# Splitting the MLP of a decode step into four column groups that overlap across engines

## The chip, the cores and the metric

The kernel runs on one core of a Trainium2 chip. A core has engines that each run their own instruction stream in order: TensorE (matrix multiplies and transposes, written PE in the profile, with its weight loads as PEld), VectorE (DVE), ScalarE (ACT), GpSimd (POOL) and SyncE (SP). They wait for each other on semaphores. DMA queues move data between main memory (HBM) and the on-chip SBUF; TensorE writes its results to PSUM. The metric is the device time of one execution in microseconds (us). Five executions of the kernel before have a median of 883.75 us (882.21 to 885.1).

## The reference

One decode step (one token each for 8 sequences) through two identical layers. x has 8 rows of 640 values. Each layer is an attention with a key and value cache and then an MLP, both with a layer norm ahead and a residual add behind:

```python
W = min(4096, max(256, Sk // 4))          # 1024 of 4096 cached positions
q = (x @ wq)                              # 32 heads of 128
scores = einsum("bhqd,bhkd->bhqk", q, k) * (Dh ** -0.5)
o = einsum("bhqk,bhkd->bhqd", softmax(scores), v)
return o @ wo

def _B_ref(x, w1, b1, w2, b2):
    y = _layernorm(x, axis=-1)
    h = _gelu(einsum("bsd,df->bsf", y, w1) + b1)     # tanh form, F = 1728
    return einsum("bsf,fd->bsd", h, w2) + b2
...
x = x + _A_ref(_layernorm(x, axis=-1), A_k_cache, A_v_cache, A_wq, A_wo)
x = x + _B_ref(_layernorm(x, axis=-1), B_w1, B_b1, B_w2, B_b2)
x = x + _A_ref(_layernorm(x, axis=-1), A_k_cache, A_v_cache, A_wq, A_wo)
x = x + _B_ref(_layernorm(x, axis=-1), B_w1, B_b1, B_w2, B_b2)
```

Both layers use the same weights and the same caches. The caches' last 1024 positions amount to some 134 MB, which are read once per attention.

## The kernel before

The program emits attention, MLP, attention, MLP (`emit_A`, `emit_B`, lines 733 to 736). Each `emit_` function adds blocks to the engines' streams, and on each engine the order of the blocks is the order of execution. Every dependency is a semaphore wait written by hand: `S_DVM`, `S_ACM` and `S_PEM` count finished steps of VectorE, ScalarE and TensorE in the parts outside the attention's loop.

**Attention** (lines 285 to 648). It walks 32 chunks, each being 8 heads of one sequence, with 2 MB of K and 2 MB of V. There are three K buffers and two V buffers. K transfers are issued by SyncE (L592), V transfers by ScalarE (L509). In each chunk VectorE computes the scores of six heads by a multiply and reduce (L346), and TensorE those of two, by transposing K (L413), a copy on ScalarE (L531) and a product (L423). ScalarE takes the exponentials, TensorE multiplies with V (L447). The layer starts with the queries (L366, evacuated by L499, spread over the partitions by L380 and L519) and ends with the output projection L631 and the residual add L640. SyncE starts the K transfers of layer 2 as soon as the projection L631 of layer 1 is done, so before the MLP. The first V transfer of layer 2 comes behind the second L499 in ScalarE's stream.

**Layer norm** (`emit_ln_yt`, L221 to L283) is shared by both kinds of layer. Two sums on ScalarE (L227, L229), five tiny steps on VectorE, a logarithm and an exponential with their table loads (L248, L250), the normalised rows YBF (L262), five transposes (L271) and their copy to YTS (L278). Then VectorE builds SELB, eight selector matrices (L281), which the attention's broadcast L380 uses. The function returns VectorE's count after SELB, and TensorE waits for that count before it uses YTS.

**MLP** (`emit_B`, L650 to L731). In the order in which it runs:
- L662: y @ w1 into HP, 8 rows of 1728 fp32 values in PSUM. Five chunks of the inner size 640 accumulate, in column pieces of at most 512; twenty matmuls.
- L671 to L677 on VectorE, over all 1728 columns: add B1 (result UB in bf16), square, multiply by 0.044715 and add 1, multiply by UB.
- L683 on ScalarE: tanh. L690 and L692 on VectorE: half of tanh plus a half, times UB, into HBF.
- L701: fourteen transposes bring HBF's 128-column pieces to partitions (HT_PS). L708 and L709 copy them to HTS.
- L720: HTS @ w2 into O2_PS, 8 rows of 640; fourteen matmuls of 512 columns and then fourteen of 128.
- L728 adds the residual, L730 adds B2.

Each step waits for the whole of the one before. UB, SELB and the layer norm's scratch lie in the same memory (UF). HP lies in PSUM tensor P4, HT_PS in TPS; MPS is used only by the attention.

Of the kernel before, what the change touches and what calls it, by code (L numbers as in the profile page):

```python
# [8 lines left out]
BF16 = mybir.dt.bfloat16  # L9
I32 = mybir.dt.int32  # L10
ALU = mybir.AluOpType
ACTF = mybir.ActivationFunctionType
# [16 lines left out]
def bass_interleave_layers__sliding_block_cached__mixer_channel_mlp__decode_kernel(  # L29
# [13 lines left out]
    B, Sq, D = A_x.shape  # L43
# [11 lines left out]
    DC = D // 128  # L55
# [21 lines left out]
    with es:  # L77
# [76 lines left out]
        HT_PS = TPS[:, 64:64 + FC * 8]  # L154
        TPOSB = TPS[:, 256:384]
        TPOS = [TPOSA, TPOSB]
        DEN_PS = [ACC[0:1, 512:512 + H * J], ACC[0:1, 768:768 + H * J]]
        WO_PS = ACC[0:8, 0:D]
        O2_PS = ACC[0:8, 0:D]
# [58 lines left out]
            S_DVM.inc(v.tensor_single_scalar(IDENT128[:, :], IOTA128[:, :], 0, ALU.is_equal))  # L218
        DVM_IDENT = S_DVM.count

        def emit_ln_yt(xin, x_ready_waits):  # L221
            @block.scalar
            def _(sc):
                for s, cval in x_ready_waits:
                    sc.wait_ge(s.handle, cval)
                sc.wait_ge(S_ACM.handle, S_ACM.count)
                S_ACM.inc(sc.activation(JUNK[:, :], xin[0:B, :], ACTF.Identity, accum_out=STAT[:, 0:1]))  # L227
                sc.wait_ge(S_ACM.handle, S_ACM.count)
                S_ACM.inc(sc.activation(JUNK[:, :], xin[0:B, :], ACTF.Square, accum_out=STAT[:, 1:2]))  # L229
            acm_stat = S_ACM.count  # L230

            @block.vector
            def _(v):
                v.wait_ge(S_ACM.handle, acm_stat)
                S_DVM.inc(v.tensor_scalar(STAT[:, 2:3], STAT[:, 0:1], 1.0 / D, None, ALU.mult))
                S_DVM.inc(v.tensor_scalar(STAT[:, 3:4], STAT[:, 1:2], 1.0 / D, None, ALU.mult))
                v.wait_ge(S_DVM.handle, S_DVM.count)
                S_DVM.inc(v.tensor_tensor(STAT[:, 4:5], STAT[:, 2:3], STAT[:, 2:3], ALU.mult))
                v.wait_ge(S_DVM.handle, S_DVM.count)
                S_DVM.inc(v.tensor_tensor(STAT[:, 5:6], STAT[:, 3:4], STAT[:, 4:5], ALU.subtract))  # L240
                v.wait_ge(S_DVM.handle, S_DVM.count)
                S_DVM.inc(v.tensor_scalar(STAT[:, 6:7], STAT[:, 5:6], 1e-5, None, ALU.add))
            dvm_var = S_DVM.count

            @block.scalar
            def _(sc):
                sc.wait_ge(S_DVM.handle, dvm_var)
                S_ACM.inc(sc.activation(STAT[:, 6:7], STAT[:, 6:7], ACTF.Ln))  # L248
                sc.wait_ge(S_ACM.handle, S_ACM.count)
                S_ACM.inc(sc.activation(STAT[:, 6:7], STAT[:, 6:7], ACTF.Exp, scale=-0.5))  # L250
            acm_sqrt = S_ACM.count

            @block.vector
            def _(v):
                v.wait_ge(S_ACM.handle, acm_sqrt)
                S_DVM.inc(v.scalar_tensor_tensor(STAT[:, 7:8], STAT[:, 2:3], -1.0, STAT[:, 6:7], ALU.mult, ALU.mult))
            dvm_nmr = S_DVM.count

            @block.scalar
            def _(sc):  # L260
                sc.wait_ge(S_DVM.handle, dvm_nmr)
                S_ACM.inc(sc.activation(YBF[0:B, :], xin[0:B, :], ACTF.Identity, bias=STAT[:, 7:8], scale=STAT[:, 6:7]))  # L262
            acm_y = S_ACM.count

            @block.tensor
            def _(t):
                t.wait_ge(S_ACM.handle, acm_y)
                t.wait_ge(S_DVM.handle, DVM_IDENT)
                ins = None
                for c in range(DC):  # L270
                    ins = t.transpose(YT_PS[:, c * 8:c * 8 + 8], YBF[0:B, c * 128:(c + 1) * 128], IDENT128[0:B, 0:B])  # L271
                S_PEM.inc(ins)
            pem_yt = S_PEM.count

            @block.vector
            def _(v):
                v.wait_ge(S_PEM.handle, pem_yt)
                S_DVM.inc(v.tensor_copy(YTS[:, :, 0:B], YT_PS[:, 0:DC * 8].rearrange("p (c b) -> p c b", c=DC)))  # L278
                ins = None
                for b in range(B):  # L280
                    ins = v.tensor_copy(SELB[0:8, b, :], IDENT128[0:8, b:b + 1].to_broadcast([8, 128]))  # L281
                S_DVM.inc(ins)
            return S_DVM.count  # L283

        def emit_A(xin, xout, x_ready):
# [362 lines left out]
            return dvm_x  # L648

        def emit_B(xin, xout, x_ready):  # L650
            dvm_yts = emit_ln_yt(xin, x_ready)

            @block.tensor
            def _(t):
                t.wait_ge(S_DVM.handle, dvm_yts)
                t.wait_ge(WA_W1[0].handle, WA_W1[1])
                ins = None
                n0 = 0
                while n0 < F:
                    n1 = min(n0 + 512, F)  # L660
                    for c in range(DC):
                        ins = t.matmul(HP[0:8, n0:n1], YTS[:, c, :], W1[:, c, n0:n1], start=(c == 0), stop=(c == DC - 1))  # L662
                    n0 = n1
                S_PEM.inc(ins)
            pem_hp = S_PEM.count

            @block.vector
            def _(v):
                v.wait_ge(S_PEM.handle, pem_hp)
                v.wait_ge(WA_B[0].handle, WA_B[1])  # L670
                S_DVM.inc(v.tensor_tensor(UB[0:B, :], HP[0:B, 0:F], B1[0:B, :], ALU.add))  # L671
                v.wait_ge(S_DVM.handle, S_DVM.count)
                S_DVM.inc(v.tensor_tensor(VBF[0:B, :], UB[0:B, :], UB[0:B, :], ALU.mult))
                v.wait_ge(S_DVM.handle, S_DVM.count)
                S_DVM.inc(v.tensor_scalar(VBF[0:B, :], VBF[0:B, :], 0.044715, 1.0, ALU.mult, ALU.add))
                v.wait_ge(S_DVM.handle, S_DVM.count)
                S_DVM.inc(v.tensor_tensor(VBF[0:B, :], VBF[0:B, :], UB[0:B, :], ALU.mult))  # L677
            dvm_v = S_DVM.count

            @block.scalar  # L680
            def _(sc):
                sc.wait_ge(S_DVM.handle, dvm_v)
                S_ACM.inc(sc.activation(VBF[0:B, :], VBF[0:B, :], ACTF.Tanh, scale=GELU_C))  # L683
            acm_s = S_ACM.count

            @block.vector
            def _(v):
                v.wait_ge(S_ACM.handle, acm_s)
                with nc.allow_low_precision("gelu bf16 intermediates"):
                    S_DVM.inc(v.tensor_scalar(VBF[0:B, :], VBF[0:B, :], 0.5, 0.5, ALU.mult, ALU.add))  # L690
                v.wait_ge(S_DVM.handle, S_DVM.count)
                S_DVM.inc(v.tensor_tensor(HBF[0:B, :], VBF[0:B, :], UB[0:B, :], ALU.mult))  # L692
            dvm_h = S_DVM.count

            @block.tensor
            def _(t):
                t.wait_ge(S_DVM.handle, dvm_h)
                ins = None
                for k in range(FC):
                    cols = 128 if k < FC - 1 else F_LAST  # L700
                    ins = t.transpose(HT_PS[0:cols, k * 8:k * 8 + 8], HBF[0:B, k * 128:k * 128 + cols], IDENT128[0:B, 0:B])  # L701
                S_PEM.inc(ins)
            pem_ht = S_PEM.count

            @block.vector
            def _(v):
                v.wait_ge(S_PEM.handle, pem_ht)
                S_DVM.inc(v.tensor_copy(HTS[:, 0:FC - 1, 0:B], HT_PS[:, 0:(FC - 1) * 8].rearrange("p (k b) -> p k b", k=FC - 1)))  # L708
                S_DVM.inc(v.tensor_copy(HTS[0:F_LAST, FC - 1, 0:B], HT_PS[0:F_LAST, (FC - 1) * 8:FC * 8]))  # L709
            dvm_hts = S_DVM.count  # L710

            @block.tensor
            def _(t):
                t.wait_ge(S_DVM.handle, dvm_hts)
                t.wait_ge(WA_W2[0].handle, WA_W2[1])
                ins = None
                for (n0, n1) in [(0, 512), (512, D)]:
                    for k in range(FC):
                        rows = 128 if k < FC - 1 else F_LAST
                        ins = t.matmul(O2_PS[0:8, n0:n1], HTS[0:rows, k, :], W2[0:rows, k, n0:n1],  # L720
                                       start=(k == 0), stop=(k == FC - 1))
                S_PEM.inc(ins)
            pem_o2 = S_PEM.count

            @block.vector
            def _(v):
                v.wait_ge(S_PEM.handle, pem_o2)
                S_DVM.inc(v.tensor_tensor(xout[0:B, :], xin[0:B, :], O2_PS[0:B, 0:D], ALU.add))  # L728
                v.wait_ge(S_DVM.handle, S_DVM.count)
                S_DVM.inc(v.tensor_tensor(xout[0:B, :], xout[0:B, :], B2[0:B, :], ALU.add))  # L730
            return S_DVM.count  # L731

        dvm_x1 = emit_A(XT[0], XT[1], [(S_GD, 16)])
# [43 lines left out]
```

The softmax here doesn't subtract the row's maximum and nothing guards it: scores larger than these inputs give would overflow.

## Time and profile before

| | |
|---|---|
| median of 5 executions | 883.75 us (882.21 to 885.1) |
| span of the profiled execution | 879.6 us |
| busy, share of the span | TensorE 532.2 us (60%), VectorE 726.3 (83%), ScalarE 353.4 (40%) |
| data moved by DMA | 290.16 MB, mean 330 GB/s |
| first MLP: W1's first matmul to the last add's end | 424.59 to 447.32 us |
| second MLP: the same | 854.39 to 877.33 us |
| layer norm of the first MLP, up to W1's start | 417.06 to 424.59 us |

How to read it: the page divides the span into 40 slices of 22 us. A digit is an engine's busy share of a slice in tenths; PEclk is the granted TensorE clock in tenths of full speed; GB/s is what the DMA engines moved. The chain of work that ended last follows each instruction back to what released it. In a list of instructions or of the chain, the first number is the start, the second the duration in us, and "x20" a group of twenty. A matmul's row lasts longer than its share of the stream since matmuls are pipelined. In a table of stretches come, after the stretch's length, the busy time of each engine with its count of instructions (TensorE, weight loads, VectorE, ScalarE, GpSimd, or one engine alone), the granted clock, the DMA share and GB/s.

### The profile page before, as it was taken

How to read it: one execution, taken by the hardware profiler on the slowest of the kernel's cores; microseconds unless marked ns; L12 is line 12 of the kernel's file. 1: busy time of each engine (PE TensorE's matmuls, PEld its weight loads, DVE VectorE, ACT ScalarE, POOL GpSimd, SP SyncE). 2: the span in 40 equal slices, each digit the busy share in tenths (PEclk: the TensorE clock that was granted, in tenths of full speed). 3: DMA queues.
4: the chain of work that ended last, by engine and by line, in shares of the span. 5: the costliest groups of instructions: out<-in, count | busy, mean ns of one | idle time of the engine just before them, and what ended most of it. 6: DMA issues, size and time to landing. Idle time of an engine off the chain costs nothing.

```text
span 879.6 us, 23392 instructions
## 1 busy us (share of the span) xinstructions
PE 532.2 (60%) x6964; PEld 304.8 (35%) x6964; DVE 726.3 (83%) x6264; ACT 353.4 (40%) x1337; POOL 4.0 (0%) x11
## 2 busy tenths in 40 slices
PE   0866656565656566656358776656565656566364
PEld 0433333333333333333114443333333333333221
DVE  1499999999999999992319999999999999999513
ACT  3454444444444444430235544444444444444120
POOL 1000000000000000000000000000000000000000
PEclk9955555555555555557666555555555555555577
DMA  9999999999999999993706999999999999999700
GB/s 370 381 386 386 385 376 381 364 372 362 373 369 372 363 378 376 373 351 106 280 18 238 356 386 386 386 383 376 364 363 369 372 363 373 362 365 376 253 1 0
DMA packets 143071, 290.16 MB, mean 330 GB/s; under 512 B 2256, under 2 KB 10464, under 8 KB 142304
## 3 DMA queue, kind: packets, MB, share of 16 engines
q1 hardware_dynamic: 74864, 144.72, 44.8%
q10 hardware_dynamic: 67248, 139.50, 43.5%
q0 software_dynamic: 832, 4.44, 1.3%
q8 instruction: 55, 0.90, 0.4%
q14 instruction: 72, 0.59, 0.2%
HBM read 288.64 MB, written 0.01 MB: 328 GB/s over the span
## 4 chain that ended last, share of the span: by engine, by line
DVE 79%; DMA 7%; PE 6%; issue 4%; ACT 3%; DVEq 1%; ACTq 0%
DVE SCRD L346 72%; DVE MLPSCR L346 4%; DMA WQ<-in_A_wq_dram 3%; PE ACC L631 2%; DMA KVALL<-in_A_v_cache_dram 2%; PE P L662 1%; DMA KVALL<-in_A_k_cache_dram 1%; PE ACC L720 1%; DMA KVALL<-in_A_wo_dram 1%; DVE DSUM L317 1%; DVE RDEN L319 1%; DVEq L345 0%; DVE UF L671 0%; ACT L250 0%; ACT L248 0%
## 5 line engine op out<-in xcount | busy, mean ns | idle before, releaser
L346 DVE CUSTOM_DVE_ANT_0 SCRD<-KVALL,QBCB 128x128 bf16<-128x128 bf16 x3072 | 683.2, 285 | 57.9 <-DMA KVALL<-in_A_k_cache_dram 20.3
L346 DVE DVE_READ_ACCUMULATOR2_ANT MLPSCR<- 128x1 f32 x3072 | 246.2, 80 | 0.2
L531 ACT ACTIVATE KTS<-P 128x128 bf16<-128x128 bf16 x512 | 141.8, 277 | 161.8 <-PE P L413 57.5
L519 ACT ACTIVATE QBCB<-P 128x512 bf16<-128x512 f32 x128 | 69.4, 594 | 218.7 <-DVE MLPSCR L346 212.9
L380 PE MATMUL P<-QROWS,UF 8*128 8x512 bf16 x128 | 62.4, 577 | 137.8 <-ACT QBCB L519 136.4
L531 ACT ACTIVATE KTS<-TPS 128x128 bf16<-128x128 bf16 x512 | 139.7, 273 | 4.4
L413 PE MATMUL TPS<-IDENT,KVALL 128*128 128x128 bf16 x512 | 139.9, 273 | 0.0
L413 PE MATMUL P<-IDENT,KVALL 128*128 128x128 bf16 x512 | 138.8, 271 | 0.5 <-DMA KVALL<-in_A_k_cache_dram 0.5
L447 PE MATMUL MPS<-MLPSCR,KVALL 128*128 128x1 bf16 x4096 | 119.0, 165 | 25.4 <-DMA KVALL<-in_A_v_cache_dram 24.5
L423 PE MATMUL P<-QCOL,KTS 128*128 128x1 bf16 x512 | 91.5, 187 | 57.4 <-ACT KTS L531 56.0
L447 PEld LDWEIGHTS MPS<-MLPSCR,KVALL 128*128 128x128 bf16 x4096 | 114.2, 104 | 30.2 <-issue 19.7
L423 PE MATMUL ACC<-QCOL,KTS 128*128 128x1 bf16 x512 | 91.6, 187 | 51.8 <-ACT KTS L531 50.5
L423 PEld LDWEIGHTS P<-QCOL,KTS 128*128 128x128 bf16 x512 | 53.7, 105 | 119.5 <-ACT KTS L531 110.7
L423 PEld LDWEIGHTS ACC<-QCOL,KTS 128*128 128x128 bf16 x512 | 53.7, 105 | 114.9 <-ACT KTS L531 106.2
L380 PEld LDWEIGHTS P<-QROWS,UF 8*128 8x128 bf16 x128 | 12.2, 99 | 165.3 <-issue 142.6
L413 PEld LDWEIGHTS P<-IDENT,KVALL 128*128 128x128 bf16 x512 | 59.6, 116 | 27.5 <-issue 26.9
L413 PEld LDWEIGHTS TPS<-IDENT,KVALL 128*128 128x128 bf16 x512 | 59.9, 117 | 0.0
L366 PE MATMUL P<-WQ,YTS 128*8 128x512 bf16 x80 | 21.8, 437 | 11.1 <-DMA WQ<-in_A_wq_dram 9.7
L227 ACT ACTIVATE UF<-XT 8x640 f32<-8x640 f32 x4 | 2.9, 735 | 53.1 <-DVE XT L640 39.5
L631 PE MATMUL ACC<-KVALL,OTS 128*8 128x128 bf16 (+1 forms) x128 | 20.7, 327 | 3.3 <-DMA KVALL<-in_A_wo_dram 2.1
L271 PE MATMUL TPS<-IDENT,YBF 8*128 8x8 bf16 x20 | 1.2, 167 | 34.0 <-ACT YBF L262 34.0
L550 ACT ACTIVATE MLPSCR<-MLPSCR 128x48 bf16<-128x48 f32 x64 | 15.6, 244 | 15.2 <-DVE MLPSCR L346 15.2
(65 smaller groups left out, 172.2 us busy)
## 6 DMA issues: line engine op xcount, KB each, us to landing
KVALL<-in_A_k_cache_dram SPq DMA_DIRECT2D x64, 2048.0 KB, 17.6
KVALL<-in_A_v_cache_dram ACTq DMA_DIRECT2D x64, 2048.0 KB, 18.4
KVALL<-in_A_wo_dram SPq DMA_DIRECT2D x4, 1920.0 KB, 12.7
WQ<-in_A_wq_dram ACTq DMA_DIRECT2D x1, 5120.0 KB, 22.1
KVALL<-in_A_wo_dram SPq DMA_DIRECT2D x2, 1280.0 KB, 16.8
W<-in_B_w_dram POOLq DMA_DIRECT2D x1, 2160.0 KB, 16.9
W<-in_B_w_dram POOLq DMA_DIRECT2D x1, 2080.0 KB, 23.9
W<-in_B_w_dram POOLq DMA_DIRECT2D x1, 80.0 KB, 23.6
```

The source lines that it names most:

```text
L317: S_DVM.inc(v.tensor_reduce(out=DSUM[:, :], in_=den[0:1, 0:H * J].rearrange("p (h j) -> p h j", j=J), axis=AXX, op=ALU.add))
L319: v.reciprocal(out=RDEN[:, (pb - bt0) * H:(pb - bt0 + 1) * H], in_=DSUM[:, :])
L346: ins = v.tensor_tensor_reduce(out=SCRD[:, slot, :], in0=k_buf[:, hh, j, :], in1=QBCB[gc % 2][:, hh, :], scale=SCALE, scalar=0.0, op0=ALU. ...
L366: ins = t.matmul(QRPS[gq % 2][0:8, 0:QG * Dh], YTS[:, c, :], WQ[:, c, qg * QG * Dh:(qg + 1) * QG * Dh], start=(c == 0), stop=(c == DC - 1))
L380: S_QBM.inc(t.matmul(QPS[qb % 2][:, :], SELB[0:8, b, :], QROWS[0:8, (g * HC + hf * QG) * Dh:(g * HC + (hf + 1) * QG) * Dh], start=True, st ...
L413: S_TP.inc(t.transpose(TPOS[n % 2][:, 0:128], k_buf[:, hh, j, :], IDENT128[:, :]))
L423: S_PQ.inc(t.matmul(SCPS[gc % 2][:, col:col + 1], KTS[n % 2][:, :], QCOL[:, h, b:b + 1], start=True, stop=True))
L447: ins = t.matmul(OTP[:, col:col + 1], v_buf[:, hh, j, :], PB[bt % 2][:, h * J + j:h * J + j + 1], start=(j == 0), stop=(j == J - 1))
L519: S_QEB.inc(sc.activation(QBCB[gc % 2][:, hf * QG:(hf + 1) * QG, :], QPS[qb % 2][:, :].rearrange("p (h d) -> p h d", h=QG), ACTF.Copy))
L531: S_KTE.inc(sc.activation(KTS[n % 2][:, :], TPOS[n % 2][:, 0:128], ACTF.Copy))
L550: S_EXP.inc(sc.activation(PB[bt % 2][:, g * HC * J:(g * HC + hdv) * J], SB[bt % 2][:, g * HC * J:(g * HC + hdv) * J], ACTF.Exp))
L631: ins = t.matmul(WO_PS[0:8, n0:n1], OTS[:, h * 8:h * 8 + 8], WO(h)[:, n0:n1], start=(h == 0), stop=(h == H - 1))
```

## The change

The MLP is split into four groups of columns (512, 512, 512, 192). The aim is that the gelu of one group runs on VectorE and ScalarE while TensorE works on another, and that TensorE's second product starts before the whole gelu is done. Its parts:

- `emit_ln_yt` gets a switch, and the MLP no longer builds SELB.
- W1's matmuls keep their order, but count a semaphore after each group.
- VectorE runs the steps in the order of `ORDER_V`: F is the front (add B1, square, polynomial, product), T the tail after tanh, C the copy of the transposes. TensorE runs X (transposes of a group) and D (its products with W2, both column pieces) in the order of `ORDER_P`. ScalarE takes the tanh by group.
- The transposes alternate between TPS and MPS, so that one group's can be written while another's are copied.
- Four matmuls into MPS ahead of the first X, and seven into P4 ahead of the first D, compute nothing that is used; they are there to keep TensorE active.
- B2 is added to the residual right after the layer norm instead of at the end, so that one add is left there.

```diff
+        HT_PSS = [HT_PS, MPS.bitcast(BF16)[:, 0:FC * 8]]
...
-        def emit_ln_yt(xin, x_ready_waits):
+        def emit_ln_yt(xin, x_ready_waits, build_sel=True):
...
-                ins = None
-                for b in range(B):
-                    ins = v.tensor_copy(SELB[0:8, b, :], IDENT128[0:8, b:b + 1].to_broadcast([8, 128]))
-                S_DVM.inc(ins)
+                if build_sel:
+                    ins = None
+                    for b in range(B):
+                        ins = v.tensor_copy(SELB[0:8, b, :], IDENT128[0:8, b:b + 1].to_broadcast([8, 128]))
+                    S_DVM.inc(ins)
...
+            dvm_yts = emit_ln_yt(xin, x_ready, build_sel=False)
+
+            GCOLS = [(0, 512), (512, 1024), (1024, 1536), (1536, F)]
+
+            @block.vector
+            def _(v):
+                for s_, cval in x_ready:
+                    v.wait_ge(s_.handle, cval)
+                v.wait_ge(WA_B[0].handle, WA_B[1])
+                S_DVM.inc(v.tensor_tensor(xout[0:B, :], xin[0:B, :], B2[0:B, :], ALU.add))
+            dvm_xb = S_DVM.count
+
+            ORDER_V = [('F', 0), ('F', 1), ('T', 0), ('F', 2), ('C', 0), ('T', 1), ('F', 3), ('C', 1), ('T', 2), ('T', 3), ('C', 2), ('C', 3)]
+            ORDER_P = [('X', 0), ('D', 0), ('X', 1), ('D', 1), ('X', 2), ('X', 3), ('D', 2), ('D', 3)]
...
+                for gi, (g0, g1) in enumerate(GCOLS):
+                    for n0 in range(g0, g1, 512):
+                        n1 = min(n0 + 512, g1)
+                        for c in range(DC):
+                            ins = t.matmul(HP[0:8, n0:n1], YTS[:, c, :], W1[:, c, n0:n1], start=(c == 0), stop=(c == DC - 1))
+                    S_PEM.inc(ins)
+                    assert S_PEM.count == pU[gi]
+                for what, gi in ORDER_P:
+                    g0, g1 = GCOLS[gi]
+                    ks = range(g0 // 128, (g1 + 127) // 128)
+                    if (what, gi) == ("X", 0):
+                        for _i in range(4):
+                            t.matmul(MPS[0:8, 0:512], YTS[:, 0, :], W1[:, 0, 0:512], start=True, stop=True)
+                    if (what, gi) == ("D", 0):
+                        for _i in range(7):
+                            t.matmul(P4[0:8, 0:512], YTS[:, 0, :], W1[:, 0, 0:512], start=True, stop=True)
+                    if what == "X":
+                        t.wait_ge(S_DVM.handle, dT[gi])
+                        for k in ks:
+                            cols = min(128, F - k * 128)
+                            ins = t.transpose(HT_PSS[gi % 2][0:cols, k * 8:k * 8 + 8], HBF[0:B, k * 128:k * 128 + cols], IDENT128[0:B, 0:B])
+                        S_PEM.inc(ins)
+                        assert S_PEM.count == pX[gi]
+                    else:
+                        t.wait_ge(S_DVM.handle, dC[gi])
+                        if gi == 0:
+                            t.wait_ge(WA_W2[0].handle, WA_W2[1])
+                        for k in ks:
+                            rows = min(128, F - k * 128)
+                            for (n0, n1) in [(0, 512), (512, D)]:
+                                ins = t.matmul(O2_PS[0:8, n0:n1], HTS[0:rows, k, :], W2[0:rows, k, n0:n1], start=(k == 0), stop=(k == FC - 1))
                 S_PEM.inc(ins)
...
+                for what, gi in ORDER_V:
+                    g0, g1 = GCOLS[gi]
+                    u, w = UB[0:B, g0:g1], VBF[0:B, g0:g1]
+                    if what == "F":
+                        v.wait_ge(S_PEM.handle, pU[gi])
+                        S_DVM.inc(v.tensor_tensor(u, HP[0:B, g0:g1], B1[0:B, g0:g1], ALU.add))
+                        v.wait_ge(S_DVM.handle, S_DVM.count)
+                        S_DVM.inc(v.tensor_tensor(w, u, u, ALU.mult))
+                        v.wait_ge(S_DVM.handle, S_DVM.count)
+                        S_DVM.inc(v.tensor_scalar(w, w, 0.044715, 1.0, ALU.mult, ALU.add))
+                        v.wait_ge(S_DVM.handle, S_DVM.count)
+                        S_DVM.inc(v.tensor_tensor(w, w, u, ALU.mult))
+                        assert S_DVM.count == dF[gi]
+                    elif what == "T":
+                        v.wait_ge(S_ACM.handle, a0 + gi + 1)
+                        with nc.allow_low_precision("gelu bf16 intermediates"):
+                            S_DVM.inc(v.tensor_scalar(w, w, 0.5, 0.5, ALU.mult, ALU.add))
+                        v.wait_ge(S_DVM.handle, S_DVM.count)
+                        S_DVM.inc(v.tensor_tensor(HBF[0:B, g0:g1], w, u, ALU.mult))
+                        assert S_DVM.count == dT[gi]
+                    else:
+                        v.wait_ge(S_PEM.handle, pX[gi])
...
+                        S_DVM.inc(ins)
+                        assert S_DVM.count == dC[gi]
...
+                for gi, (g0, g1) in enumerate(GCOLS):
+                    sc.wait_ge(S_DVM.handle, dF[gi])
+                    S_ACM.inc(sc.activation(VBF[0:B, g0:g1], VBF[0:B, g0:g1], ACTF.Tanh, scale=GELU_C))
...
                 v.wait_ge(S_PEM.handle, pem_o2)
-                S_DVM.inc(v.tensor_tensor(xout[0:B, :], xin[0:B, :], O2_PS[0:B, 0:D], ALU.add))
-                v.wait_ge(S_DVM.handle, S_DVM.count)
-                S_DVM.inc(v.tensor_tensor(xout[0:B, :], xout[0:B, :], B2[0:B, :], ALU.add))
+                v.wait_ge(S_DVM.handle, dvm_xb)
+                S_DVM.inc(v.tensor_tensor(xout[0:B, :], xout[0:B, :], O2_PS[0:B, 0:D], ALU.add))
```

More of the change, by code (lines that the diff above doesn't have):

```diff
@@ L650, in emit_B @@
         def emit_B(xin, xout, x_ready):
-            dvm_yts = emit_ln_yt(xin, x_ready)
+            dvm_yts = emit_ln_yt(xin, x_ready, build_sel=False)
[9 more added lines that the diff above has]
+            ORDER_P = [('X', 0), ('D', 0), ('X', 1), ('D', 1), ('X', 2), ('X', 3), ('D', 2), ('D', 3)]
+            NFRONT, NTAIL = (4, 2)
+            n = S_DVM.count
+            dF, dT, dC = {}, {}, {}
+            for what, gi in ORDER_V:
+                n += dict(F=NFRONT, T=NTAIL, C=1)[what]
+                dict(F=dF, T=dT, C=dC)[what][gi] = n
+            n = S_PEM.count + len(GCOLS)
+            pU = {gi: S_PEM.count + gi + 1 for gi in range(len(GCOLS))}
+            pX = {}
+            for what, gi in ORDER_P:
+                if what == "X":
+                    n += 1
+                    pX[gi] = n
+            a0 = S_ACM.count
             @block.tensor
@@ L656, in _ @@
                 t.wait_ge(WA_W1[0].handle, WA_W1[1])
[L657 to L671, printed above, removed]
-                v.wait_ge(S_DVM.handle, S_DVM.count)
[L673 to L721, printed above, removed]
+                for gi, (g0, g1) in enumerate(GCOLS):
[5 more added lines that the diff above has]
+                    assert S_PEM.count == pU[gi]
@@ new lines, in _ @@
+                for what, gi in ORDER_P:
+                    g0, g1 = GCOLS[gi]
[6 more added lines that the diff above has]
+                            t.matmul(P4[0:8, 0:512], YTS[:, 0, :], W1[:, 0, 0:512], start=True, stop=True)
+                    if what == "X":
+                        t.wait_ge(S_DVM.handle, dT[gi])
[12 more added lines that the diff above has]
+                                ins = t.matmul(O2_PS[0:8, n0:n1], HTS[0:rows, k, :], W2[0:rows, k, n0:n1], start=(k == 0), stop=(k == FC - 1))
@@ L726, in _ @@
             def _(v):
+                v.wait_ge(WA_B[0].handle, WA_B[1])
+                for what, gi in ORDER_V:
+                    g0, g1 = GCOLS[gi]
[19 more added lines that the diff above has]
+                        v.wait_ge(S_PEM.handle, pX[gi])
+                        k0, k1 = g0 // 128, (g1 + 127) // 128
+                        ka = k1 if g1 % 128 == 0 else k1 - 1
+                        ins = v.tensor_copy(HTS[:, k0:ka, 0:B], HT_PSS[gi % 2][:, k0 * 8:ka * 8].rearrange("p (k b) -> p k b", k=ka - k0))
+                        if ka < k1:
+                            ins = v.tensor_copy(HTS[0:F - ka * 128, ka, 0:B], HT_PSS[gi % 2][0:F - ka * 128, ka * 8:k1 * 8])
+                        S_DVM.inc(ins)
+                        assert S_DVM.count == dC[gi]
@@ L727, in _ @@
+            @block.scalar
+            def _(sc):
+                for gi, (g0, g1) in enumerate(GCOLS):
+                    sc.wait_ge(S_DVM.handle, dF[gi])
+                    S_ACM.inc(sc.activation(VBF[0:B, g0:g1], VBF[0:B, g0:g1], ACTF.Tanh, scale=GELU_C))
+            @block.vector
+            def _(v):
                 v.wait_ge(S_PEM.handle, pem_o2)
-                S_DVM.inc(v.tensor_tensor(xout[0:B, :], xin[0:B, :], O2_PS[0:B, 0:D], ALU.add))
-                v.wait_ge(S_DVM.handle, S_DVM.count)
```

## The prediction

> **What bounds the kernel now.** I read the page's slices first. In the two attention layers the DMA queues run at 360 to 386 GB/s and VectorE is 9 tenths busy; in the two MLPs (slices 18 to 20, and the last two) nearly everything is idle.
>
> ```profile
> DVE  1499999999999999992319999999999999999513
> ...
> PEclk9955555555555555557666555555555555555577
> ...
> GB/s 370 381 386 386 385 376 381 364 372 362 373 369 372 363 378 376 373 351 106 280 18 238 356 386 386 386 383 376 364 363 369 372 363 373 362 365 376 253 1 0
> ```
>
> Then the chain that ended last, in order of time, around the first MLP (start, duration, what):
>
> ```profile
> 423.38 1.16 DVE UF L281 x8
> 424.59 6.11 PE P L662 x20
> 430.73 1.96 DVE UF L671
> 432.71 1.06 DVE MLPSCR L673
> 433.79 0.61 DVE MLPSCR L675
> 434.42 1.06 DVE MLPSCR L677
> 435.50 1.65 ACT MLPSCR L683
> 437.17 0.61 DVE MLPSCR L690
> 437.81 1.06 DVE HBF L692
> 438.91 0.66 PE TPS L701 x14
> 439.59 0.21 DVE HTS L708
> 439.92 5.71 PE ACC L720 x28
> 445.65 0.82 DVE XT L728
> 446.50 0.82 DVE XT L730
> ```
>
> One engine at a time works: 424.59 to 447.32 is 22.73 us of pure sequence. In the second MLP the same stretch runs from 854.39 to 877.33, 22.94 us, and only an output cast and its store follow. So all that is saved in the last MLP is saved at the end. For the first I had to ask whether the next attention layer would eat it. Busy time by stretch, with clock, DMA share and GB/s last:
>
> ```profile
> 416.00:434.00 18.00, 6.57 (x29) 2.27 (x25) 6.05 (x19) 5.54 (x9) 0.00 (x0) 0.72 0.94 350
> 434.00:454.00 20.00, 6.63 (x47) 2.93 (x47) 6.18 (x18) 7.19 (x10) 0.00 (x0) 0.72 0.00 0
> ```
>
> The three K buffers of layer 2 fill before 434, then the DMA stands still. The first V transfer is issued at 459.40, from ScalarE's queue after the second query evacuation (L499), which follows the MLP. So an earlier MLP end moves the whole V and K stream of layer 2 by as much; even 9 us earlier, its start near 450 lies after K's landing.
>
> The clock also matters. In half-microsecond stretches TensorE goes (the fourth number is the granted clock):
>
> ```profile
> 428.50:429.00 0.50, 0.50 (x3) 0.50 1.06 393
> ...
> 429.50:430.00 0.50, 0.50 (x4) 1.00 1.05 385
> ...
> 436.50:437.00 0.50, 0.00 (x0) 0.50 0.00 0
> ...
> 442.50:443.00 0.50, 0.50 (x3) 0.59 0.00 0
> 443.00:443.50 0.50, 0.50 (x4) 1.00 0.00 0
> ```
>
> It is at half clock for the first 4.7 us of W1, rises, falls during the 8.2 us gelu gap, and W2 starts at half clock again.
>
> **What the skill says.** "TensorE: Matmul & The Clock Gate", Part 1: a free-running activity window of about 3.4 us sets the clock; a busy window gives full clock and an idle one takes it back. The trace agrees: the changes come near 429.25, 436.08 and 442.9, two windows of 3.41 us apart each time. Where a window was 38% busy (859.3 to 862.75, in the second MLP) the clock fell, where 42% busy (429.25 to 432.67) it held. "VectorE: DVE Perf Modes", the perf-mode tier table: tensor_tensor takes one element per cycle with PSUM, two in bf16 SBUF; tensor_scalar four. The trace agrees: 1.945, 1.047 and 0.600 us for the same 1728 columns.
>
> **The change, part by part.**
>
> *Selector copies left out of the MLP.* L281 has eight copies of 207 ns that only attention needs, yet W1 waits for them. The YTS copy ends at 423.47, and W1 could start about 0.05 later, at 423.52 instead of 424.59: 1.07 us saved per MLP, all on the path.
>
> *B2 added early.* One 8x640 add of 0.82 us plus 0.03 leaves the end; it now runs after the YTS copy, while VectorE waits at least 2 us for the first W1 group. Cost nothing, and its semaphore wait at the end has long been met.
>
> *Four column groups.* Costs of VectorE operations on 512 and 192 columns aren't in the trace; I interpolate. PSUM add: 1.945 at 1728 (L671) and 0.809 at 640 (L728) give 0.141 + 1.044 ns a column: 0.675 and 0.341. For bf16 I take the 8x1 rows as the fixed part (0.148 for L238, 0.142 for L242): products 0.414 and 0.247, tensor_scalar 0.278 and 0.193. Tanh, from 1.642 (L683) and 0.202 (L248): 0.629 and 0.362. Dependent steps on VectorE lie 0.035 apart in the chain. Hence
> - F (add, square, polynomial, product): 0.675 + 0.414 + 0.278 + 0.414 + 4 x 0.035 = 1.92; last group 1.17.
> - T (half tail, product): 0.278 + 0.414 + 0.07 = 0.76; last group 0.51.
> - C (copy of the transposes): 0.18 from L278 (0.179) plus 0.035 = 0.21; last group, with two copies, 0.28.
>
> The fixed parts are paid four times: VectorE's work per MLP rises from 6.6 to about 10.7 us, the four F being 6.9, the T 2.8, the C 0.9. The gain is that it overlaps W1, tanh and W2.
>
> TensorE: cold matmuls of 512 columns start 0.427 apart (weight loads at 425.40, 425.83 and on); warm, 30 of L366 took 6.64, so 0.22; a warm 128-column one about 0.07 (the last 14 of L720 take 1.05). A group's result comes some 0.2 after its last start would have ended (the 512-column row means 571 ns in W1 against 0.427 spacing). Transposes: 0.167 for the first, 0.036 for each more (14 in 0.64): X of four 0.28. D of four pairs: 4 x 0.29 = 1.16; last D 0.58.
>
> **The new schedule**, with zero at W1's start, first two groups cold:
> - W1 group 0 is there at 5 x 0.427 + 0.2 = 2.33. F0 2.37 to 4.29; group 1 at 4.47, so F1 4.51 to 6.43; T0 7.20 (tanh 0 done at 4.95); F2 9.12; C0 9.33 (X0 done by about 7.8); T1 10.09; F3 11.27; C1 11.48; T2 12.24; T3 12.76.
> - D0 runs from 9.37 to 10.53, then X1. D1 waits for C1: 11.52 to 12.68. X2 queues behind D1: 12.96. C2 13.18. D2 13.22 to 14.38, D3 14.96, result 15.13. Final add 15.15 to 15.97.
>
> So VectorE is the pacing engine from 2.4 to 12.8, and TensorE only at the two ends. Waits added: X2 behind D1 (0.4, counted), C0 behind F2 (D0 waits for it; D0 then still ends before C1). The dummies: W1 ends at 5.9 to 6.8, four dummies take 0.9 warm, and X0 follows by about 7.8. Seven more take 1.5, until 9.3, about when C0 is done. They lie inside waits for T0 and C0, so cost nothing, and keep the window that ends near 9 busy. Without them the gaps before 9.3 would risk a cold D. With groups 2 and 3 warm, the clock should stay up: TensorE idles from about 10.8 to 11.5 and for 0.3 before D2, far less than half a window.
>
> Sum: 22.73 - 15.97 = 6.76 and 22.94 - 15.97 = 6.97 us, plus 2 x 1.07: 15.9 us. 883.75 - 15.9 = 867.9 us.
>
> **Bounds of what isn't shown.** Clock: if W1 were warm throughout, group 0 comes at 1.3 and F1 no longer waits: 1.3 us less per MLP, 865.3. If the phase leaves D1 cold, about 1 us more per MLP: 869.9. Gaps between VectorE steps of 0.06 rather than 0.035 over some 25 steps: 0.6 per MLP, 1.3 in all. I take the middle; the five times before spread by 1.5 us to either side. Range 864.5 to 871.5.
>
> **Rivals.**
> 1. *The clock stays half.* Then TensorE paces: W1 7.2, dummies 11 x 0.427 = 4.7, D 14 x 0.534 = 7.5, transposes 0.9, waits 0.5, tail and add 1.0: 21.8. Saves about 1 us per MLP plus 1.07: 879.5. For it: from 30 to 410 us, in attention, the clock is 0.51 although TensorE is busy for 239 of the 380 us. Against it: both MLPs reach full clock within 5 us today, and the idle stretches shrink. Chance 0.06.
> 2. *Only the last MLP counts*, layer 2 being held by its transfers: 8 us, 875.8. For it: 360 GB/s in layer 2. Against it: the zeros from 434 on; nothing is in flight that layer 2 could wait for. Chance 0.06.
> 3. *Slower: the hand-written orders interlock*, so that groups go one after another. Then 6.1 for W1, 3 x 4.0 + 2.6 for the groups' chains (F, tanh, T, X, C and hops), cold dummies 4.7, cold D 7.5, end 1.0: 33.9 against 23.9 now, 10 us worse per MLP, 904. For it: six hand-offs per group between in-order engines, and extra matmuls ahead of X0 and D0. Against it: followed by hand, every wait is met by work queued earlier. Chance 0.03.
>
> **The numbers.** My forecast's mechanism has 0.85, of which the range keeps most. Rivals 1 and 2 still end faster, so faster has 0.95, counting some for an unforeseen loss; same 0.02, slower 0.03.
>
> **What the profile would show.** Right: W1 starting some 0.05 after the YTS copy; PSUM adds of 0.68 and products of 0.41 in four groups, W1's own matmuls beneath the first; full clock from W1's third group to the last D; about 16 us from W1's start to the last add in both MLPs; no DMA in flight as MLP 1 ends and layer 2 unchanged in length. Wrong: half clock in D, VectorE operations on 512 columns over 0.5 us for the bf16 products, gaps on VectorE beyond 0.1, or a layer 2 that stretches by what MLP 1 gained.

## The result and the profile after

The changed kernel takes 865.85 us (median of 9, 864.28 to 866.78), the kernel before on the same chips 883.61 (15 executions, 881.69 to 887.74): ratio 0.9794, interval [0.9778, 0.9809], 17.8 us less. The forecast was 867.9.

The chain that ended last, in order of time, around the first MLP of the changed kernel (start, duration, what; L690 is W1, L728 the add of B1, L739 the tail after tanh, L716 W2, L763 the last add):

```profile
425.42 2.31 PE P L690 x5
427.82 0.69 DVE UF L728
428.53 0.42 DVE MLPSCR L730
...
429.71 0.61 DVE UF L728
...
431.52 0.21 DVE MLPSCR L739
...
435.53 0.25 DVE MLPSCR L734
435.92 1.25 PE ACC L716 x8
437.62 1.90 PE ACC L716 x12
439.54 0.82 DVE XT L763
```

Before, twenty W1 matmuls and 6.1 us stood ahead of the first gelu step; now five and 2.3 us. From 427.82 until C1's copy ends at 435.85 VectorE has no gap of more than 0.05, and of W2 only D1 to D3 are left on the chain. From W1's start to the last add's end it is 14.94 us (22.73 before), in the second MLP 847.69 to 862.67, 14.98 (22.94). W1 starts 0.24 after the YTS copy's start (425.18 to 425.42), where it was 1.30: 1.06 saved per MLP. Together 7.79 + 7.96 + 2.12 = 17.87 us, beside the measured 17.8; the two agree better than single executions do, which differ by 2.5 us in the changed kernel and by 6 in the one before. (The two profiled spans, 879.6 and 865.0, differ by 14.6: in that execution of the changed kernel the first attention ended 1.9 us later and the second lasted 1.3 longer. The second run with a warm W1 below shows where such differences lie.)

The stretches around the first MLP, as in the table of the kernel before (length, busy times, clock, DMA share, GB/s):

```profile
418.00:436.00 18.00, 9.82 (x55) 3.89 (x54) 10.19 (x32) 7.62 (x13) 0.00 (x0) 0.81 0.96 350
436.00:448.00 12.00, 3.71 (x32) 1.74 (x32) 4.05 (x23) 5.72 (x10) 0.00 (x0) 0.75 0.00 0
```

K's transfers still end ahead of layer 2, before 436, and next to nothing is moved until the first V transfer is issued at 452.40. The first score step of layer 2 comes at 454.6 (461.3 before), the last at 818.2 (825.1): 363.6 us against 363.8. So the earlier start went through unchanged.

### The profile page after: what moved, and what is told of

Its sections match the earlier page's. It is cut to its first block, busy times and chain, and to the rows that moved or that the text cites. A ratio compares the mean times of both kernels' runs of the same rounds, so it can differ in the third digit from the quotient of the medians.

```text
span 865.0 us, 23472 instructions
## 1 busy us (share of the span) xinstructions
PE 533.9 (62%) x6986; PEld 306.0 (35%) x6986; DVE 728.7 (84%) x6290; ACT 351.7 (41%) x1343; POOL 4.0 (0%) x11
## 3 DMA queue, kind: packets, MB, share of 16 engines
q0 software_dynamic: 832, 4.44, 1.3%
## 4 chain that ended last, share of the span: by engine, by line
DVE 78%; DMA 9%; PE 5%; issue 4%; ACT 2%; DVEq 1%; ACTq 0%
DVE SCRD L348 71%; DMA KVALL<-in_A_v_cache_dram 4%; DVE MLPSCR L348 4%; PE ACC L633 3%; DMA WQ<-in_A_wq_dram 3%; DMA KVALL<-in_A_k_cache_dram 1%; DMA KVALL<-in_A_wo_dram 1%; PE ACC L716 1%; PE MPS L449 1%; DVE DSUM L319 1%; DVE RDEN L321 1%; PE P L690 1%; DVE UF L728 1%; DVEq L347 0%; ACT L251 0%
## 5 line engine op out<-in xcount | busy, mean ns | idle before, releaser
L368 PE MATMUL P<-WQ,YTS 128*8 128x512 bf16 x80 | 23.6, 463 | 11.4 <-DMA WQ<-in_A_wq_dram 10.0
L633 PE MATMUL ACC<-KVALL,OTS 128*8 128x128 bf16 (+1 forms) x128 | 22.5, 344 | 3.8 <-DMA KVALL<-in_A_wo_dram 2.6
```

Of the source, the lines that this page charges most:

```text
L368: ins = t.matmul(QRPS[gq % 2][0:8, 0:QG * Dh], YTS[:, c, :], WQ[:, c, qg * QG * Dh:(qg + 1) * QG * Dh], start=(c == 0), stop=(c == DC - 1))
L633: ins = t.matmul(WO_PS[0:8, n0:n1], OTS[:, h * 8:h * 8 + 8], WO(h)[:, n0:n1], start=(h == 0), stop=(h == H - 1))
```

## The experiments

All times are medians of executions beside the kernel before on the same chip, with the ratio to it and its interval; the ratio takes in all executions and isn't the quotient of the two medians. "MLP" is the stretch from W1's start to the last add's end, in the two MLPs of the trace.

**The two small edits alone.** On the kernel before:

```diff
-            dvm_yts = emit_ln_yt(xin, x_ready)
+            dvm_yts = emit_ln_yt(xin, x_ready, build_sel=False)
...
+                S_DVM.inc(v.tensor_tensor(xout[0:B, :], xin[0:B, :], B2[0:B, :], ALU.add))
...
-                S_DVM.inc(v.tensor_tensor(xout[0:B, :], xin[0:B, :], O2_PS[0:B, 0:D], ALU.add))
-                v.wait_ge(S_DVM.handle, S_DVM.count)
-                S_DVM.inc(v.tensor_tensor(xout[0:B, :], xout[0:B, :], B2[0:B, :], ALU.add))
+                v.wait_ge(S_DVM.handle, dvm_xb)
+                S_DVM.inc(v.tensor_tensor(xout[0:B, :], xout[0:B, :], O2_PS[0:B, 0:D], ALU.add))
```

> The kernel before with the two small edits alone: no selector copies in the MLP, B2 added early; no column groups, no fillers. Theory: 1.07 + 0.85 us per MLP, 3.8 in all, 879.8. Rival (these two lay beside other work): 883.6, and the groups carry all 17.8.

Measured: 880.59 us, ratio 0.9942 [0.9923, 0.9961], that is 5.1 us less, with an interval of 3.4 to 6.8. It excludes the rival; the expected 3.8 us of 883.6 are a ratio of 0.9957, inside. So the two edits lie on the path, and their 3.8 us would be about a fifth of the whole. In the trace W1 starts 0.24 us after the YTS copy's start in both MLPs, as it should, but the MLPs are hardly shorter (22.82 and 22.67 us, before 22.73 and 22.94): W2 took 7.11 and 5.97 us there, before 5.71 and 5.78, and the second W1 6.6 instead of 6.2, so in this execution longer stretches at half clock ate most of what the early add saved.

**The clock alone.** The same, plus thirty fillers between W1 and the transposes:

```diff
+                for _i in range(30):
+                    t.matmul(MPS[0:8, 0:512], YTS[:, 0, :], W1[:, 0, 0:512], start=True, stop=True)
                 t.wait_ge(S_DVM.handle, dvm_h)
```

> The same as the run with the two small edits, plus thirty filler matmuls (results unused) between W1 and the transposes, 6.6 us at full clock in an 8.2 us gap. It gives the clock's share without any overlap. Theory: W2 falls from 5.7 to about 4.2 us, 1.5 us per MLP, so 3 us below the run without fillers: 876.8. Rival (the gain of the column groups is mostly the warm clock, not the overlap): over 6 us below. Rival (the clock doesn't hold): the same as without fillers.

Measured: 876.86 us, ratio 0.9894 [0.9872, 0.9917], 3.7 us below the run without fillers. In the first MLP W2 took 4.24 us, at full clock; in the run without fillers 7.11 and 5.97. The second MLP shows how narrow it is. TensorE's wait ahead of the transposes was the same in both:

```profile
439.25 0.59 PE L712 MATMUL TPS<-IDENT,HBF 8*128 8x8 bf16 x14 [1.75 <-DVE HBF L701]
...
865.01 0.59 PE L712 MATMUL TPS<-IDENT,HBF 8*128 8x8 bf16 x14 [1.75 <-DVE HBF L701]
```

TensorE in half-microsecond stretches of the second (busy time, instructions, granted clock, DMA share, GB/s):

```profile
863.00:863.50 0.50, 0.26 (x2) 1.00 0.00 0
863.50:864.00 0.50, 0.00 (x0) 1.00 0.00 0
...
865.00:865.50 0.50, 0.49 (x14) 1.00 0.00 0
865.50:866.00 0.50, 0.14 (x2) 1.00 0.00 0
866.00:866.50 0.50, 0.50 (x2) 0.60 0.00 0
866.50:867.00 0.50, 0.50 (x2) 0.50 0.00 0
```

The fillers ended 1.75 us before the transposes, the clock fell at 866.1, just as W2 had begun, and W2 took 5.93 us. A warm clock without overlap is thus worth 1.5 to 2.9 us per MLP when it holds (4.24 us for W2 against 5.71 in the kernel before and 7.11 in the run without fillers), far from the 7 that the change saves per MLP beyond the two small edits.

**The changed kernel without its fillers.**

```diff
-                    if (what, gi) == ("X", 0):
-                        for _i in range(4):
-                            t.matmul(MPS[0:8, 0:512], YTS[:, 0, :], W1[:, 0, 0:512], start=True, stop=True)
-                    if (what, gi) == ("D", 0):
-                        for _i in range(7):
-                            t.matmul(P4[0:8, 0:512], YTS[:, 0, :], W1[:, 0, 0:512], start=True, stop=True)
```

> The changed kernel without its eleven filler matmuls. Theory (the fillers cost nothing and hold the clock): TensorE has 0.25 us of work between the end of W1 at 5.3 and D0 at 8.6 us after W1's start, so in most phases of the clock window D0 and perhaps D1 run at half clock, about 1 to 2 us more per MLP: 867.5 to 870. Rival (fillers don't matter, the chain is VectorE's): within 0.5 us of the changed kernel's 865.9.

Measured: 869.61 us, ratio 0.9819 [0.9795, 0.9843]. That interval overlaps the changed kernel's, so the trace has to decide. D0 and D1 in the first MLP of this run (start, duration, the eight matmuls of a group):

```profile
434.02 1.25 PE L710 MATMUL ACC<-W,HTS 128*8 128x512 bf16 x8 [1.64 <-DVE HTS L741]
...
435.81 2.30 PE L710 MATMUL ACC<-W,HTS 128*8 128x512 bf16 x8 [0.36 <-DVE HTS L741]
```

and TensorE's clock there (the fourth number):

```profile
434.00:435.00 1.00, 0.98 (x7) 1.00 1.06 391
435.00:436.00 1.00, 0.64 (x7) 0.83 0.76 274
436.00:437.00 1.00, 1.00 (x5) 0.50 0.00 0
```

The clock falls just ahead of D1, which takes 2.30 instead of 1.25 us; the second MLP has the same 2.30. The MLPs take 16.22 and 16.29 us, 1.3 more than with fillers. Theory confirmed, with D1 rather than D0 as the group hit.

**The changed MLP in layer 1 only**, the former MLP (old `emit_B`) in layer 2:

```diff
-        dvm_x4 = emit_B(XT[1], XT[0], [(S_DVM, dvm_x3)])
+        dvm_x4 = emit_B_old(XT[1], XT[0], [(S_DVM, dvm_x3)])
```

> The changed MLP in layer 1, the MLP of the kernel before in layer 2. Theory (layer 2's transfers start earlier by what MLP 1 gains): 7.8 + 1.06 us less than before, 874.7. Rival (layer 2 is held by its transfers, only the last MLP counts): 883.6.

Measured: 875.17 us, ratio 0.988 [0.9858, 0.9902]. The rival (ratio 1) is out: an MLP in the middle counts in full. In this run too layer 2's score steps take from 453.7 to 817.4, 363.7 us.

**The changed kernel again, as a yardstick for the next three.**

> The changed kernel itself, as a yardstick on the same chip for the three runs beside it. Both theories: 0.979 of the kernel before, and both MLPs 14.9 to 15.0 us from W1's start to the last add's end, whatever the phase of the clock.

Measured: 864.82 us, ratio 0.9777 [0.9753, 0.9801]. MLPs 15.38 and 14.95. The first was longer because the clock rose late: W1 took 6.75 us there, and the second F waited 0.18 for its group. So "whatever the phase" was too strong, by 0.4.

**Two groups instead of four.**

```diff
-            GCOLS = [(0, 512), (512, 1024), (1024, 1536), (1536, F)]
+            GCOLS = [(0, 1024), (1024, F)]
...
+            ORDER_V = [('F', 0), ('F', 1), ('T', 0), ('T', 1), ('C', 0), ('C', 1)]
+            ORDER_P = [('X', 0), ('D', 0), ('X', 1), ('D', 1)]
```

> Two column groups (1024 and 704) in place of four; VectorE's order F0 F1 T0 T1 C0 C1, the fillers kept. Theory (what pays is the overlap; the fixed part of 0.14 us per instruction is cheap): F0 can only start with ten W1 matmuls done, at 4.3 us, and D0 only after all four front and tail steps, near 12; the end comes at about 17.0 us instead of 14.9, so 4 us slower than the changed kernel, 870. Rival (the fixed parts, paid four times, cost what the overlap brings): VectorE saves 13 instructions of 0.14, 1.8 us per MLP, and the kernel is 3 to 4 us faster, 862.

Measured: 874.14 us, ratio 0.9889 [0.9861, 0.9916], some 9 us slower than the yardstick. MLPs 18.51 and 19.83 us, where 17.0 was expected. Most of the rest is the fillers' doing, in lines of the second MLP:

```profile
860.01 3.15 PE L701 MATMUL P<-W,YTS 128*8 128x512 bf16 x7
860.39 0.17 DVE L747 COPY HTS<-TPS 128x64 bf16<-128x64 bf16 x1
862.96 2.39 PE L716 MATMUL ACC<-W,HTS 128*8 128x512 bf16 x16
```

The copy that D0 (L716) waits for is done at 860.56, but the seven fillers, at half clock here, hold TensorE until 862.96: 2.4 us on the path. In the first MLP they ran at full clock and held D0 for 0.9 us (copy done at 435.50, D0 at 436.44). Without them the two MLPs would have taken 17.6 and 17.4 us, so coarser groups cost some 2.5 us per MLP by this reckoning, and the rest of the 9 us is the fillers' and the executions' scatter. Fillers are free only in the gap for which they were counted.

**VectorE's steps interleaved**, two fillers instead of seven ahead of D0:

```diff
+            ORDER_V = [('F', 0, 0), ('F', 0, 1), ('F', 0, 2), ('F', 0, 3),
+                       ('F', 1, 0), ('F', 1, 1), ('T', 0, 0), ('F', 1, 2), ('T', 0, 1), ('F', 1, 3),
...
-                        for _i in range(7):
+                        for _i in range(2):
```

> The changed kernel with VectorE's steps interleaved: a tail step or a copy of another group between two steps that depend on each other, and two fillers instead of seven ahead of D0. Same work. Theory (two independent VectorE steps start 0.07 us before the former ends, dependent ones 0.035 after it, which is why the prediction's chain was 1 us too long): some six dependent borders per MLP become independent, and the queue behind D0 gets shorter; 0.5 to 0.75 us per MLP, 864.5. Rival (the early start isn't due to independence): no change, or slower by what the finer order makes TensorE wait, 866 to 867.

Measured: 865.91 us, ratio 0.9788 [0.9764, 0.9811]; MLPs 14.06 and 14.05, 0.9 shorter, but no shorter time. Two things were changed here, the order and the count of fillers, so the 0.9 isn't the order's alone by this run. Run once more:

> The interleaved order once more: its trace showed both MLPs 0.9 us shorter, its time 1.1 us longer than the changed kernel's beside it. Theory (the 2.6 us between them lay in layer 2's last wait for its weights and in the clock's phase, both chance): ratio near 0.976, and in the trace the stretch from the last score step to the output projection back near 10.3 us from 11.9. Rival (the shorter MLP is given back in layer 2): ratio 0.979 again and the stretch long again.

Measured: 864.25 us, ratio 0.979 [0.9765, 0.9816]; MLPs 14.05 and 14.78 (W1 6.60, late clock). The stretch from the last score step to the projection, 11.9 us in the former trace, was 10.8, between the 10.3 of the theory and the rival's. The ratio is the one that the rival named. So the shorter MLP is in the traces, the gain of 1 to 2 us in time isn't shown.

**ScalarE's own gelu** (its table function replaces the formula's steps), no fillers:

```diff
-                    S_ACM.inc(sc.activation(VBF[0:B, g0:g1], VBF[0:B, g0:g1], ACTF.Tanh, scale=GELU_C))
+                    S_ACM.inc(sc.activation(HBF[0:B, g0:g1], UB[0:B, g0:g1], ACTF.Gelu_apprx_tanh))
...
-            ORDER_P = [('X', 0), ('D', 0), ('X', 1), ('D', 1), ('X', 2), ('X', 3), ('D', 2), ('D', 3)]
+            ORDER_P = [('X', 0), ('X', 1), ('D', 0), ('X', 2), ('D', 1), ('X', 3), ('D', 2), ('D', 3)]
```

> The changed kernel with ScalarE's own tanh-gelu in place of the six VectorE steps of square, polynomial, products and tail; VectorE keeps the add of B1 and the copies; TensorE's order X0 X1 D0 X2 D1 X3 D2 D3 and no fillers. Theory (VectorE paces the changed MLP, so taking its work away leaves TensorE's): W1 5.3, X0 and X1 0.5, hand-off 0.3, D 4.2, X2 and X3 0.4, tail and add 1.0: 11.7 us instead of 14.9, 6.4 us less in all, 859.5. Rival (a table load of 1.28 us before the first gelu and another before the next layer norm's first step lie on the path): 2 to 5 us of it lost, 862 to 865.

Measured: 859.84 us, ratio 0.9715 [0.9689, 0.9742]; MLPs 11.08 and 11.67. VectorE was what paced the changed MLP. The fillers and TensorE's order went with it, so the time is that of all three together. The one table load it adds to an MLP (1.28 us) ran at 425.04, beside the transposes and W1, and the next layer norm showed no more loads than before.

**A warm W1**: the changed kernel with fillers during the MLP's layer norm.

```diff
+                for _i in range(warm):
+                    t.matmul(MPS[0:8, 0:512], YTS[:, 0, :], W1[:, 0, 0:512], start=True, stop=True)
                 t.wait_ge(S_ACM.handle, acm_y)
...
+            dvm_yts = emit_ln_yt(xin, x_ready, build_sel=False, warm=28)
```

> The changed kernel with 28 filler matmuls (6.2 us at full clock, results unused) on TensorE during the layer norm of each MLP, where it idles 6.8 us after the output projection. Theory (the first W1 group at half clock is what the schedule starts from): group 0 comes at 1.3 instead of 2.4 us, VectorE's chain starts as much earlier, 1.1 to 1.3 us per MLP less, 863.3 by the changed kernel's 865.9, ratio about 0.976. Rival (something else than group 0 paces): W1 is faster in the trace, but the last add comes no earlier, 865.9.

Measured: 865.9 us, ratio 0.9786 [0.976, 0.9812], inconclusive: two executions took 861.5 and 862.1, four 865.9 to 866.1. In the trace (of the one at 861.5) W1 took 3.81 us and the MLPs 13.88 and 13.87, 1.1 shorter as expected. It was run again for a trace of a longer execution:

> The changed kernel with a warm W1 once more: of six executions two took 861.5 to 862.1 us, as the shorter MLPs in its trace ask for, and four 865.9 to 866.1. Both theories: MLPs of 13.9 us in the trace again. Theory (the 4 us lie in the attention, and have nothing to do with the MLP): a trace of a longer execution shows them before the first MLP or between the two. Rival (the earlier MLP is given back in layer 2): then in the stretch from the first to the last score step of layer 2, or in the wait for the output projection's weights, longer than the 363.6 to 364.4 and 9.6 to 11.9 of the traces so far.

Measured: 864.27 us (861.58 to 866.16), ratio 0.9766 [0.9737, 0.9796]; this time the traced execution took 865.6. The output projection in layers 1 and 2 (minimum, median and maximum of a matmul in ns, first and last start), first of the shorter, then of the longer execution:

```profile
L637 PE MATMUL ACC<-KVALL,OTS x64: 219/299/631, 405.8 to 416.0; 128*8 128x512 bf16 x32, 128*8 128x128 bf16 x32
...
L637 PE MATMUL ACC<-KVALL,OTS x64: 219/299/631, 825.9 to 835.9; 128*8 128x512 bf16 x32, 128*8 128x128 bf16 x32
```

```profile
L637 PE MATMUL ACC<-KVALL,OTS x64: 219/299/631, 406.8 to 417.4; 128*8 128x512 bf16 x32, 128*8 128x128 bf16 x32
...
L637 PE MATMUL ACC<-KVALL,OTS x64: 219/299/634, 828.9 to 840.1; 128*8 128x512 bf16 x32, 128*8 128x128 bf16 x32
```

Of the 4.1 us between the two, 1.4 had come by the end of layer 1's attention, which is the same code in both kernels: its projection began 1.0 later and took 0.4 more. Another 2.3 came at the end of layer 2's: the wait from the last score step to the projection was 11.7 instead of 10.4 us, the projection 11.2 instead of 10.1 from first to last start. The MLPs and the score stretches (363.7 and 363.8) were alike. The projection's part is the clock's: it rose 2.9 us after layer 2's projection had begun in the shorter execution, 5.2 us after in the longer. So the first of the rival's two places, the score steps, is cleared. The second isn't: 1.2 us of the difference are in the wait for the projection's weights. The 11.7 lie within the range of the earlier traces, but over all fourteen traces the six whose MLPs were made shorter than the changed kernel's have waits of 10.4 to 11.9 us, the other eight of 9.6 to 10.4. Whether part of such a gain is given back there, or the two groups differ by chance, stays open. By these two runs' times the gain of a warm W1 alone isn't shown either: their ratios (0.9786 and 0.9766) hardly differ from those of the changed kernel (0.9794 and 0.9777).

**Both, the fastest version.** ScalarE's gelu with warm layer norms, in layer 2's attention too:

```diff
+            dvm_yts = emit_ln_yt(xin, x_ready, warm=28 if a else 0)
```

> The run with ScalarE's gelu plus the same fillers in the layer norms of both MLPs and of layer 2's attention. Theory: TensorE paces this MLP, so a warm W1 is worth 0.7 to 1.3 us in each; the ten query matmuls ahead of layer 2's first V transfer fall from 4.4 to 2.3 us; together 4 us under that run's 859.8: 856. Rival (layer 2 gives back what it is started earlier): 858.

Measured: 853.57 us, ratio 0.9664 [0.9638, 0.969], faster than both kernels, and 6.3 us under the run with ScalarE's gelu (4.5 by the two ratios), where 4 were expected. So the rival is out, and here warm layer norms show in the time. MLPs 9.77 and 9.76. Its first MLP:

```profile
424.00 3.81 PE L694 MATMUL P<-W,YTS 128*8 128x512 bf16 x20 [0.27 <-DVE YTS L283]
425.36 0.68 DVE L726 TENSOR_TENSOR UF<-P,B 8x512 bf16<-8x512 f32 x1 [0.69 <-PE P L694]
426.07 0.63 ACT L742 ACTIVATE HBF<-UF 8x512 bf16<-8x512 bf16 x1 [1.36 <-DVE UF L726]
...
428.27 1.25 PE L714 MATMUL ACC<-W,HTS 128*8 128x512 bf16 x8 [0.17 <-DVE HTS L732]
...
429.63 1.25 PE L714 MATMUL ACC<-W,HTS 128*8 128x512 bf16 x8
...
431.04 1.88 PE L714 MATMUL ACC<-W,HTS 128*8 128x512 bf16 x12
```

TensorE now idles only 0.17 us between W1 and the last D, and the ten query matmuls ahead of layer 2's first V transfer take 2.32 us instead of 4.43.

## Why the prediction was right

**The chain and its shift through layer 2.** Both MLPs were a pure sequence, and what they lost, the kernel lost. Layer 2's score steps took 363.6 to 364.4 us in the traces of the changed kernel and of all twelve runs above, 363.8 before. Rival 2 is refuted by the run with one changed MLP.

**The small edits.** 1.07 per MLP was forecast for the selectors, 1.06 measured; the early add ran from 425.28 to 426.08, under W1's first group.

**The interpolated costs.** PSUM add 0.675 forecast, 0.67 to 0.68 measured; product 0.414 and 0.41; tensor_scalar 0.278 and 0.28; tanh 0.629 and 0.63; D of eight matmuls 1.16 and 1.25 with the tail of the last one. From D1's start to the end the schedule said 4.45 us and the trace has 4.44.

**The term that was off: the borders on VectorE.** Forecast end 15.97, measured 14.94. F0 ended at 4.29 after W1's start, as forecast. The difference arises between there and C1: C1 was to start at 11.27, and started at 435.70, 10.28 after W1's start. The prediction put 0.035 us between any two VectorE steps, as the serial chain of before shows. In the timeline of the changed kernel:

```profile
428.98 0.28 DVE L732 TENSOR_SCALAR MLPSCR<-MLPSCR 8x512 bf16<-8x512 bf16 x1
429.30 0.41 DVE L734 TENSOR_TENSOR MLPSCR<-MLPSCR,UF 8x512 bf16<-8x512 bf16 x1
429.64 0.67 DVE L728 TENSOR_TENSOR UF<-P,B 8x512 bf16<-8x512 f32 x1
429.74 0.63 ACT L757 ACTIVATE MLPSCR<-MLPSCR 8x512 bf16<-8x512 bf16 x1 [4.94 <-DVE MLPSCR L734]
430.34 0.41 DVE L730 TENSOR_TENSOR MLPSCR<-UF 8x512 bf16<-8x512 bf16 x1
...
435.53 0.25 DVE L734 TENSOR_TENSOR MLPSCR<-MLPSCR,UF 8x192 bf16<-8x192 bf16 x1
435.70 0.15 DVE L747 COPY HTS<-MPS 128x32 bf16<-128x32 bf16 x1
```

L734 needs L732's result and starts 0.04 after its end. L728 belongs to the next group, needs nothing of L734, and starts 0.07 before L734's end. Seven borders from F0's end to C1's start are of this kind, about 0.1 each: 0.7 us. The other 0.2 to 0.3 is mainly F1's wait for group 1, which the prediction had at half clock to the end and which came in time. The interleaved run turned more borders into independent ones, and where nothing else is waited for they start 0.04 to 0.08 before the former's end.

That 865.85 lies in the range of 864.5 to 871.5 is in part luck. Its lower side was drawn for a warm W1, which didn't occur; for the borders the prediction allowed only longer gaps, to 0.06 us, and they were shorter.

**The fillers.** "Cost nothing" held: the seven ended at 434.08 and D0's copy (L747) at 434.06.

```profile
432.41 1.67 PE L701 MATMUL P<-W,YTS 128*8 128x512 bf16 x7
...
433.91 0.15 DVE L747 COPY HTS<-TPS 128x32 bf16<-128x32 bf16 x1
...
434.12 1.25 PE L716 MATMUL ACC<-W,HTS 128*8 128x512 bf16 x8
```

"Without them a cold D" held too, at D1, 1.3 us per MLP. Rival 1 (clock at half) didn't occur: it was 1.00 from within W1's second group to the last D in both MLPs. The prediction's other bound, a warm W1 worth 1.3 us per MLP, measures 1.1 in the traces.

**Rival 3** (an interlock) left no trace: W2's groups follow each other within 0.55 us (D0's end at 435.37 to D1's start), and on the chain that ended last the only such stretch is the 0.45 us between 437.17 and 437.62, in which X2, X3 and their copies run.

By the traces, 3.8 of the 17.8 us are the small edits and about 2.6 the fillers' clock (16.25 against 14.96 per MLP). The remaining 11.4 are what the groups bring without fillers: the overlap, and with it a shorter idle stretch of TensorE, for D0 ran at full clock without fillers too. These two are not taken apart.

## What to carry to other kernels

When one engine at a time works in a stage, split it by columns and count what the split costs per instruction from two shapes of the same row: fixed part and slope. Here the fixed part of some 0.14 us per instruction, paid four times, raised VectorE's work per MLP from 6.6 to 9.7 us, and the kernel still became 11 us faster by the groups. Then ask again which engine paces: moving the gelu from VectorE to ScalarE was worth another 5 to 6 us. Fillers for the clock are free only in a gap that has been counted, and the idle layer norm ahead of a matmul stage is such a gap too: with them W1 still started 0.23 to 0.24 us after the YTS copy's start.

## What the runs showed of the hardware

- Consecutive VectorE instructions: some 0.04 us after the former's end where the next waits for its result, 0.07 before it where it doesn't, even with a wait on an older count in between. The Trainium skill, "VectorE: DVE Perf Modes", section "The DRAIN you can't avoid", has the next operation wait for the pipe to empty and says that one that isn't held starts earlier; the traces put the difference at 0.1 us.
- A TensorE gap of 1.75 us, with fourteen small transposes and 0.36 us more of waiting behind it, was enough to lose the full clock in one MLP and not in the other of the same execution. Of the 3.41 us up to where the clock fell (862.69 to 866.10) TensorE was busy for 1.30; of the 3.41 us around the same gap in the first MLP (436.02 to 439.43), where the clock stayed up, for 1.67. The 38% and 42% that the prediction read from two such stretches draw no line, though: in the run without fillers the clock fell after stretches with 1.44 and 1.55 us, 42 and 45%, transposes counted. The times of one kernel spread by where the clock changes: the same 64 projection matmuls took 10.2 to 11.8 us.
- A switch to ScalarE's gelu table costs one load of 1.28 us per MLP, and none of the layer norm's other steps needed a further one.
